# Gated linear attention and a token/channel mixer on one core: batch 0's mixer input made directly in transposed form, residuals joined on TensorE, and a new instruction order

## The chip, the core and the metric

The kernel runs on one core of a Trainium2 chip. The metric is the device time of one execution in microseconds (us); lower is better. The input is the same draw in every run.

## The reference

Two stages follow each other. The first is a gated recurrence with a state of 48 x 48 for each of 4 batches and 8 heads, over 768 steps:

```python
state = alpha[:, :, t, :, None] * state + k[:, :, t] (outer) v[:, :, t]
y[:, :, t] = q[:, :, t] @ state
```

The outputs of the 8 heads are laid side by side, so that each batch has an x of 768 tokens x 384 channels. The second stage is a mixer on each batch:

```python
xt = x.transpose(0, 2, 1)
h = np.maximum(xt @ w_tok1, 0.0) @ w_tok2          # 768 -> 256 -> 768, over tokens
u = x + h.transpose(0, 2, 1)
h2 = np.maximum(u @ w_ch1, 0.0) @ w_ch2            # 384 -> 1536 -> 384, over channels
return u + h2
```

All inputs and the output are float32; the matmuls run in bfloat16.

## The kernel before

**Tiling.** The recurrence is computed in blocks of 256 tokens: 3 blocks for each batch, 12 in all, numbered 0 to 11. A block puts pairs of neighbouring tokens on the 128 partitions. For each block the kernel loads alpha, k, q and v (`ld_at`, `ld_kt`, `ld_qt`, `ld_vt`, 384 KB each), takes logarithms and cumulative sums (`ln`, `cum`/`cumw`), exponentials (`E`, `IE`), scales k and q (`kk`, `qq`, L702), transposes them on TensorE (`trk`, `trq`, L717 or L721) and evicts them to SBUF (`evk`, `evq`), multiplies keys by queries (`G0`, `G1`, L651), applies the causal mask (`mask0`, `mask1`, L771, VectorE), and multiplies by v (`y`). What earlier tokens contribute through the carried state comes in as two small groups of matmuls into the same two PSUM banks, `ia` and `ib`. Between them stands a fence (`fe`, L823): ScalarE or VectorE copies four numbers out of the banks. In the kernel before the order in a block is `y`, `ia`, `fe`, `ib`; then the two 128-token halves are evicted as x (`x0`, `x1`). The state itself goes through `K` (TensorE), `sa` (VectorE) and `sm` (VectorE or GpSimd).

**Mixer of a batch.** `t1` (12 matmuls of 128x384, L843), relu (`ht`), `t2` (L850; for batch 0 with one identity matmul on x ahead of each pair, L848, which is how the residual enters; for the other batches the residual is added by VectorE, L854), eviction of u (`u`), transposes of u (`up`, 18 of 128x128, L861), their eviction (`ut`), then 24 groups of three matmuls (`c1`, L869) with a relu each (`rt`), then 24 groups of three (`c2`, L874), the residual sum (`o`, L878, VectorE) and the store (`st`).

**Order.** The instruction order is not found by a scheduler at build time. The string `ORDER` lists every operation once, with a letter for its engine (t TensorE, s ScalarE, v VectorE, g GpSimd, y SyncE's DMA queue, n left out); each engine runs its own operations in that order. A planner (`Plan.decode`) walks the list with estimated durations only to hand out buffers and PSUM banks, so a bank's next writer waits for the reader that the planner put before it. Operations whose names begin with `f` and a digit, and `pad`, are matmuls on zeros that compute nothing. They can be left out (n) or kept (t).

**Weights.** w_tok1, w_tok2, w_ch1 and w_ch2 come in pieces of 384 KB (`ldw_wt1`, `ldw_wt2`, `ldw_wc1`, `ldw_wc2`; L620), interleaved with the loads of the blocks on the one SyncE queue, and each is cast to bfloat16 (`cw_...`, L759 or L758). The mixer of batch 0 cannot start a stage before its weights are cast.

**Shared port.** VectorE and GpSimd operations that share a port are chained by a dependency (`shared`, L745).

Of the kernel before, what the change touches and what calls it, by code (L numbers as in the profile page):

```python
# [9 lines left out]
BF16 = mybir.dt.bfloat16  # L10
# [53 lines left out]
class Plan:  # L64
# [29 lines left out]
    def decode(self):  # L94
# [9 lines left out]
        dma_in, ring = 2500.0, [0.0] * 3  # L104
# [5 lines left out]
        for o in self.order:  # L110
# [61 lines left out]
            if o.dma is not None:  # L172
                kind, dur, lead, tail = o.dma
                s = max(st + lead, dma_in)
                dma_in = s + dur * (1.0 if s < 16000.0 else LATER)
                o.end = dma_in + tail + (lag(s) if kind == "i" else 0.0)
                if kind == "i":
                    ring = ring[1:] + [dma_in]
                    free[e] = max(free[e], ring[0] - 600.0)
# [19 lines left out]
LATER = 1.06  # L199


def lag(s):
    return (0.0 if s < 12500.0 else 600.0 if s < 14000.0 else 1600.0 if s < 20000.0 else 2400.0 if s < 30000.0 else
            3300.0 if s < 58000.0 else 1500.0)

# [6 lines left out]
IN_NS, WT_NS, OUT_NS = 1250.0, 1020.0, 580.0  # L212
# [4 lines left out]
    "tpk": 2, "tpq": 2, "gtm": 2, "tmp": 3, "ss": 5, "x": 14, "ht": 4, "u": 13, "ut": 2, "rt": 24, "o": 3,  # L217
}
WIDE = (0, 1, 2)
JOIN = (0,)  # L220
# [6 lines left out]
def build(g):  # L227
# [8 lines left out]
    def attention(n):  # L236
# [31 lines left out]
        else:  # L268
# [15 lines left out]
        kk = O("kk", either(dve(768), pool_tt(768)), 5, writes=[pkk], reads=[kt, IE], port=True, preds=k_in + [e2],  # L284
               emit=lambda e: g.scaled(e, pkk, kt, IE, wide))
        qq = O("qq", either(dve(768), pool_tt(768)), 5, writes=[pkq], reads=[qt, E], port=True, preds=q_in + [e1],
               emit=lambda e: g.scaled(e, pkq, qt, E, wide))
# [4 lines left out]
        bk, bq, tpk, tpq = V(kind), V(kind), V("tpk"), V("tpq")  # L292
        shape = [128] * 8 if full else [64] * 8
        trk = O("trk", pe(shape), 8, writes=[bk], reads=[pkk], preds=[kk] + fill("trk", bk),
                emit=lambda e: g.tr(bk, pkk, full, 2, 1), mode=mode, mm=8 if full else 16)
        trq = O("trq", pe(shape), 8, writes=[bq], reads=[pkq], preds=[qq] + fill("trq", bq),
                emit=lambda e: g.tr(bq, pkq, full, 2 if full else 1, 1 if full else 4), mode=mode,
                mm=8 if full else 16)
        evk = O("evk", either(dve(1024, True), act(1024)), 9, writes=[tpk], reads=[bk], preds=[trk],
                emit=lambda e: g.trev(e, tpk, bk, full))  # L300
        evq = O("evq", either(dve(1024), {"ACT": (1190.0, 1310.0)}), 9, writes=[tpq], reads=[bq], preds=[trq],
                emit=lambda e: g.trevq(e, tpq, bq, full))
        gtm = V("gtm")
        masks = []
        for sl in range(2):
            gp = V("pair")
            G = O(f"G{sl}_", pe([128] * 4), 10 + sl, writes=[gp], reads=[tpk, tpq], preds=[evk, evq] + fill(f"G{sl}", gp),
                  emit=lambda e, sl=sl, gp=gp: g.gmm(gp, tpk, tpq, sl, full), mode="G", mm=16)
            masks.append(O(f"mask{sl}_", dve(1024), 12 + sl, writes=[gtm], reads=[gp], preds=[G],
                           emit=lambda e, sl=sl, gp=gp: g.mask(gtm, gp, sl)))  # L310
        nst = 2 if k < NB - 1 else 1
        kp = V("pair")
        KO = O("K", {"PE": (276.0 if nst == 2 else 140.0, 420.0)}, 9.5, writes=[kp], reads=[pkk, vb], preds=[kk, vc] + fill("K", kp),
# [3 lines left out]
        for hf in range(nst):  # L317
# [4 lines left out]
            else:  # L322
# [7 lines left out]
        yi = O("y", pe([48] * 16), 14, writes=[yp], reads=[gtm, vb], preds=masks + [vc] + fill("y", yp),  # L330
               emit=lambda e: g.ymm(yp, gtm, vb), mode="R", mm=32)
        use = [st for st in states[:2] if st]
        ia = O("ia", pe([48] * 4), 15, writes=[yp], reads=[tpq] + [v for v, _ in use], preds=[yi] + [o for _, o in use],
               emit=lambda e: g.inter(yp, tpq, [st and st[0] for st in states[:2]], 0, full), mode="R", mm=8)
        fe = O("fe", either(act(4), dve(4)), 15, reads=[yp], preds=[ia], emit=lambda e: g.fence(e, yp))
        io = O("ib", pe([48] * 4), 15, writes=[yp], reads=[tpq] + [v for v, _ in use], preds=[fe],
               emit=lambda e: g.inter(yp, tpq, [st and st[0] for st in states[:2]], 1, full), mode="R", mm=8)
        for hf in range(2):
            x = V("x")
            xo = O(f"x{hf}_", either(act(384), dve(384)), 16, writes=[x], reads=[yp], preds=[io],  # L340
                   emit=lambda e, hf=hf, x=x: g.xev(e, x, yp, hf))
            xs[(b, 2 * k + hf)] = (x, xo)
# [12 lines left out]
    def mixer(b):  # L355
# [20 lines left out]
        us = []  # L376
        for i in range(NS):
            bank, u = V("one"), V("u")
            add = b in JOIN
            o = P.op(f"t2_{b}_{i}", pe([384] * (3 if add else 2)), m0 + (1900 + 330 * i) * sc, writes=[bank],  # L380
                     reads=[h for h, _ in hts] + ([x[i][0]] if add else []),
                     preds=[h for _, h in hts] + [wl[("wt2", z)] for z in range(2)] + ([x[i][1]] if add else []),
                     emit=lambda e, i=i, bank=bank, add=add: g.tok2(bank, i, [h for h, _ in hts], add and x[i][0]),
                     mm=3 if add else 2)
            uo = P.op(f"u_{b}_{i}", either(act(384), dve(384)) if add else dve(384), m0 + (1950 + 330 * i) * sc,
                      writes=[u], reads=[bank] + ([] if add else [x[i][0]]), preds=[o],
                      emit=lambda e, i=i, bank=bank, u=u, add=add:
                      g.xev(e, u, bank, 0) if add else g.uadd(u, bank, x[i][0]))
            us.append((u, uo))
        ut = V("ut")  # L390
        uts = []
        for p in range(3):
            bank = V("one")
            o = P.op(f"up_{b}_{p}", pe([128] * 6), m0 + (3900 + 340 * p) * sc, writes=[bank],
                     reads=[us[2 * p][0], us[2 * p + 1][0]], preds=[us[2 * p][1], us[2 * p + 1][1]],
                     emit=lambda e, p=p, bank=bank: g.utr(bank, us[2 * p][0], us[2 * p + 1][0]), mm=6)
            eo = P.op(f"ut_{b}_{p}", either(dve(768, True), act(768)), m0 + (3950 + 340 * p) * sc, writes=[ut],
                      reads=[bank], preds=[o], emit=lambda e, p=p, bank=bank: g.utev(e, ut, bank, p))
            uts.append(eo)
        rts = []  # L400
        for mc in range(NDC):
            rt = V("rt")
            ro = []
            for half in range(2):
                bank = V("one")
                o = P.op(f"c1_{b}_{mc}_{half}", pe([384] * 3), m0 + (4900 + 975 * mc + 487 * half) * sc, writes=[bank],
                         reads=[ut], preds=uts[0:2 + half] + [wl[("wc1", mc // 2)]],
# [5 lines left out]
        for i in range(NS):  # L413
# [4 lines left out]
            for tag, c0, c1 in [("", 0, 256), ("b", 256, HD)] if last and i == 0 else [("", 0, HD)]:  # L418
                bank, prev, n = V("one"), None, c1 - c0
                late = 9900.0 * (last and i == 0) + 400.0 * (c0 > 0)  # L420
                for q4 in range(4):
# [4 lines left out]
                                emit=lambda e, q4=q4, c0=c0, c1=c1, bank=bank, i=i: g.ch2(bank, i, q4, rts, c0, c1))  # L426
                oo = P.op(f"o_{b}_{i}{tag}", dve(n), at + (2000 + late) * sc, writes=[o_],
                          reads=[bank, us[i][0]], preds=[prev],
                          emit=lambda e, c0=c0, c1=c1, bank=bank, i=i, o_=o_: g.oadd(o_, bank, us[i][0], c0, c1))
# [25 lines left out]
f1G1_1n ld_at0y pad64_t pad32_n f1cumw_2n f0cumw_0n f1G0_0n f2trk_0n f2cumw_0n f2G0_0n f1cumw_0n ln0s cumw0t  # L455
f2trq_2n f1G0_1n f0cumw_2n f1cumw_1n f1G1_0n ld_at1y ln1s pad16_t ld_kt0y f0trq_0n f0cumw_1n f2G1_1n f2G1_0n
f2cumw_1n cumw1t f1trk_0t IE0s kk0v ld_qt0y E0s qq0v E1s Et1s f2K_0n f2y_1n ld_qt1y qq1v f0trk_0n f0K_1n f0G0_0n
f2trq_1n f1trq_1n f0K_2n ld_kt1y f0trq_2n ld_vt0y ld_at2y Et0s f0trq_1n f1trk_1n f0K_0n ld_vt1y trk0t f1trq_0t
IE1s f2G0_2n f2trq_0n ld_qt2y trq0t evq0s ld_kt2y f2trk_1t trq1t f0trk_1t ldw_wt10y ld_vt2y f1trk_2n f0y_0n kk1v
evk0v f0G1_1n trk1t ld_at3y ld_kt3y f2K_2n f2trk_2n evq1s vb0g ldw_wt11y ld_qt3y evk1v ldw_wt21y f1y_1n f0G1_2n  # L460
f2G0_1n G0_0t mask0_0v f0G1_0n G1_0t f1K_0n K0t f0G0_1n G0_1t f2y_2n f0y_1n s0_0v sa1_0v f0trk_2n f1trq_2n
mask1_0v f2cumw_2t f1K_1n sm1_0g ln2s cumw2t vb1g f2G1_2n f1y_0n G1_1t mask0_1v ldw_wt20y mask1_1v E2s f2y_0n
y0t ia0t fe0s ib0t Et2s x0_0s IE2s f0G0_2n f2K_1t K1t f0y_2n x1_0s qq2g trq2t ldw_wc15y ldw_wc14y sa0_1v sm0_1v
# [62 lines left out]
class Emit:  # L526


    def __init__(self, tc, ctx, q, k, v, alpha, w, out):
# [48 lines left out]
        for t, base in ((self.mk, 0), (mkb, 128)):  # L578
            gp.affine_select(out=t, in_=t, compare_op=ALU.is_ge, fill=0.0, base=base,
                             pattern=[[-1, 2], [1, 128]], channel_multiplier=-2)  # L580
# [352 lines left out]
```

## Time and profile before

| what | value |
|---|---|
| median of 5 runs | 171.29 us (170.55 to 172.52) |
| profiled execution, its own time | 171.29 us |
| its span (first to last instruction) | 169.6 us; 1.7 us lie around it |
| TensorE busy | 161.4 us (95%) |
| VectorE / ScalarE / GpSimd busy | 118.6 / 88.2 / 55.8 us |
| HBM read / written | 25.17 MB / 4.72 MB |

PE is TensorE's matmul side, PEld its weight loads, DVE VectorE, ACT ScalarE, POOL GpSimd, SP and SPq SyncE and its DMA queue. "L651" is line 651 of the kernel. A busy TensorE is counted from the start of a matmul to its modelled end; matmuls overlap, so that a stage of small matmuls can look busy while it is not at its peak. "PEclk" is the share of the full TensorE clock that was granted. The view by windows gives busy time by engine in a stretch; the chain is followed back from the last instruction to what released each step.

### The profile page before, as it was taken

How to read it: one execution, taken by the hardware profiler on the slowest of the kernel's cores; microseconds unless marked ns; L12 is line 12 of the kernel's file. 1: busy time of each engine (PE TensorE's matmuls, PEld its weight loads, DVE VectorE, ACT ScalarE, POOL GpSimd, SP SyncE). 2: the span in 40 equal slices, each digit the busy share in tenths (PEclk: the TensorE clock that was granted, in tenths of full speed). 3: DMA queues.
4: the chain of work that ended last, by engine and by line, in shares of the span. 5: the costliest groups of instructions: out<-in, count | busy, mean ns of one | idle time of the engine just before them, and what ended most of it. 6: DMA issues, size and time to landing. Idle time of an engine off the chain costs nothing.

```text
span 169.6 us, 5827 instructions
## 1 busy us (share of the span) xinstructions
PE 161.4 (95%) x2511; PEld 105.1 (62%) x2511; DVE 118.6 (70%) x212; ACT 88.2 (52%) x170; POOL 55.8 (33%) x65
## 2 busy tenths in 40 slices
PE   7868988999999999999999999999999999999993
PEld 7535655766666666756666766756666666666562
DVE  4369678798798586999988849878974526632342
ACT  3871697758875725775657792485242413310100
POOL 5004464503651157554796459702000000000000
PEclk9997899999999999999999999999999999999999
DMA  5999999999999999989972950030000000013323
GB/s 137 325 288 274 295 289 357 309 305 253 339 346 295 268 269 272 296 221 285 271 198 58 314 152 0 4 139 4 2 4 4 0 0 0 0 50 139 139 93 139
DMA packets 58777, 30.25 MB, mean 178 GB/s; under 512 B 50688, under 2 KB 58496, under 8 KB 58752
## 3 DMA queue, kind: packets, MB, share of 16 engines
q1 hardware_dynamic: 57888, 28.78, 59.2%
q10 hardware_dynamic: 864, 1.11, 1.8%
q8 instruction: 19, 0.31, 0.7%
q14 instruction: 6, 0.05, 0.1%
HBM read 25.17 MB, written 4.72 MB: 176 GB/s over the span
## 4 chain that ended last, share of the span: by engine, by line
PE 87%; DMA 3%; DVE 3%; SPq 3%; issue 1%; ACT 0%; DVEq 0%
PE ps L869 28%; PE ps L874 28%; PE ps L651 14%; PE ps L843 5%; PE ps L850 5%; DMA ld<-in_k_dram 3%; SPq L605 3%; PE ps L717 2%; PE ps L861 2%; PE ps L721 2%; DVE pkk L702 1%; DVE gtm L771 1%; PE ps L848 1%; DVE u L759 0%; ACT IE L683 0%
## 5 line engine op out<-in xcount | busy, mean ns | idle before, releaser
L874 PE MATMUL ps<-wc,rt 128*128 128x384 bf16 (+2 forms) x300 | 52.6, 320 | 0.0
L869 PE MATMUL ps<-ut,wc 128*128 128x384 bf16 x288 | 51.7, 326 | 0.0
L838 ACT ACTIVATE rt<-ps 128x384 bf16<-128x384 f32 x53 | 24.6, 494 | 27.2 <-PE ps L869 27.0
L874 PEld LDWEIGHTS <-rt 128*128 128x128 bf16 x300 | 28.1, 98 | 16.8
L869 PEld LDWEIGHTS <-wc 128*128 128x128 bf16 x288 | 26.8, 98 | 16.8
L771 DVE TENSOR_TENSOR gtm<-ps,mk 128x1024 bf16<-128x1024 f32 x24 | 28.7, 1218 | 3.8 <-PE ps L651 3.7
L840 DVE TENSOR_SCALAR rt<-ps 128x384 bf16<-128x384 f32 x43 | 22.1, 551 | 10.2 <-PE ps L869 10.0
L878 DVE TENSOR_TENSOR o<-ps,u 128x384 f32<-128x384 f32 (+2 forms) x25 | 13.1, 539 | 12.8 <-PE ps L874 10.1
L702 POOL TENSOR_TENSOR pkq<-ld,E 128x768 bf16<-128x768 f32 x7 | 12.7, 1812 | 6.0 <-DVE ld L698 4.0
L800 POOL TENSOR_TENSOR ss<-tmp,E 128x192 bf16<-128x192 f32 x12 | 6.1, 507 | 23.7 <-DVE tmp L797 14.5
L651 PE MATMUL ps<-zs 128*128 128x64 bf16 (+1 forms) x100 | 10.6, 268 | 1.8 <-DVE zs L571 1.1
L854 DVE TENSOR_TENSOR u<-ps,x 128x384 bf16<-128x384 f32 x18 | 9.2, 552 | 3.3 <-PE ps L850 3.1
L758 ACT COPY tpq<-ps 128x1024 bf16<-128x1024 bf16 x8 | 10.4, 1316 | 1.7 <-PE ps L721 1.3
L702 DVE TENSOR_TENSOR pkk<-ld,IE 128x768 bf16<-128x768 f32 x7 | 6.7, 956 | 6.2 <-ACT IE L686 3.9
L850 PE MATMUL ps<-ht,wt 128*128 128x384 bf16 x48 | 10.4, 326 | 0.0
L758 ACT CAST x<-ps 128x384 bf16<-128x384 f32 x18 | 8.1, 485 | 2.9 <-PE ps L651 2.9
L759 POOL CAST wc<-ld 128x768 bf16<-128x768 f32 x8 | 6.5, 826 | 7.9 <-DVE ld L636 4.5
L702 POOL TENSOR_TENSOR pkk<-ld,IE 128x768 bf16<-128x768 f32 x5 | 9.0, 1808 | 0.1
L843 PE MATMUL ps<-x,wt 128*128 128x384 bf16 x48 | 9.0, 327 | 0.0
L651 PE MATMUL ps<-tpq,tpk 48*64 48x128 bf16 x384 | 8.7, 221 | 0.1
L694 POOL TENSOR_TENSOR ld<-ld,ld 128x384 f32<-128x384 f32 x7 | 7.0, 999 | 4.8 <-DVE ss L800 2.9
L651 PEld LDWEIGHTS <-tpk 48*64 48x64 bf16 x384 | 6.3, 108 | 2.2 <-issue 1.5
(88 smaller groups left out, 212.6 us busy)
## 6 DMA issues: line engine op xcount, KB each, us to landing
ld<-in_alpha_dram SPq DMA_DIRECT2D x12, 384.0 KB, 5.8
ld<-in_k_dram SPq DMA_DIRECT2D x12, 384.0 KB, 5.8
ld<-in_q_dram SPq DMA_DIRECT2D x12, 384.0 KB, 5.3
ld<-in_moe_w_ch_dram SPq DMA_DIRECT2D x12, 384.0 KB, 6.1
out_dram<-o SPq DMA_DIRECT2D x18, 192.0 KB, 2.5
ld<-in_v_dram SPq DMA_DIRECT2D x14, 192.0 KB, 4.8
ld<-in_v_dram SPq DMA_DIRECT2D x5, 384.0 KB, 5.9
ld<-in_moe_w_tok_dram SPq DMA_DIRECT2D x4, 384.0 KB, 6.1
```

The costliest lines, as they stand in the source:

```text
L651: return self.pe.matmul(out, lhsT=lhsT, rhs=rhs, start=start, stop=stop, skip_group_check=True)
L702: self.shared(self.eng[e].tensor_tensor(self.t(dst)[:, :, :, 0:D], self.t(src).rearrange("p h s d -> p s h d"), bass.AP(tensor=f.tensor, o ...
L758: return self.act.copy(d, s)
L771: self.nc.vector.tensor_tensor(self.t(gtm)[:, sl, :, :], self.pair(gp).rearrange("p a (j t) -> p (a j) t", t=128), bass.AP(tensor=m.tensor ...
L838: self.act.activation(d, s, AF.Relu)
L840: self.nc.vector.tensor_scalar_max(d, s, 0.0)
L843: self.pe.matmul(self.bank(bank)[:, 0:HD], lhsT=self.wt1[:, kc, m * 128 : m * 128 + 128], rhs=self.t(x), start=(kc == 0), stop=(kc == NS - 1))
L850: self.pe.matmul(self.bank(bank)[:, 0:HD], lhsT=self.wt2[:, kc, i * 128 : i * 128 + 128], rhs=self.t(hts[kc]), start=(kc == 0 and not x), ...
L854: self.nc.vector.tensor_tensor(self.t(u), self.bank(bank)[:, 0:HD], self.t(x), ALU.add)
L869: self.pe.matmul(self.bank(bank)[:, 0:HD], lhsT=self.wc1[:, kc, mc * 128 : mc * 128 + 128], rhs=self.t(ut)[:, kc, half * 384 : half * 384 ...
L874: self.pe.matmul(self.bank(bank)[:, 0 : c1 - c0], lhsT=self.t(rts[mc][0])[:, i * 128 : i * 128 + 128], rhs=self.wc2[:, mc, c0:c1], start=( ...
L878: self.nc.vector.tensor_tensor(self.t(o)[:, c0:c1], self.bank(bank)[:, 0 : c1 - c0], self.t(u)[:, c0:c1], ALU.add)
```

## The change

Five things change together.

1. **Batch 0's u is made transposed.** For each of six pieces (half of the tokens, 128 channels) a bank gets three identity matmuls on x (`xt`), which put x transposed into it, and then two matmuls with the roles of the operands exchanged (`t2`: the hidden tile is the stationary operand, w_tok2 the moving one). One eviction writes `ut` at once. The six joins on L848, the 18 transposes `up` and the three evictions `ut` of batch 0 go away.
2. **Batch 0's second residual is joined on TensorE.** Three identity matmuls (`cr`) put u back upright into the bank in which `c2` then accumulates; `o` becomes a plain copy, which ScalarE may do as well.
3. **Carried state first.** In each block the order becomes `ib`, `fe`, `ia`, `y`, where it was `y`, `ia`, `fe`, `ib`.
4. **Block 2 in head halves.** Scaling, transposes, evictions, `G`, mask and `y` of block 2 are cut by heads instead of by token slots, so that the second half of a step overlaps the first half of the next. The number of mask operations and of matmuls stays the same; kk, qq and the evictions become twice as many of half the size.
5. **A new order** for all engines, planned with other transfer rates and delays, with another choice of zero matmuls: 12 of 128x512 instead of 20; 80 of 128x64 as before.

The core of the diff:

```diff
-LATER = 1.06
+LATER = 1.1
-IN_NS, WT_NS, OUT_NS = 1250.0, 1020.0, 580.0
+IN_NS, WT_NS, OUT_NS = 1215.0, 1050.0, 580.0
-JOIN = (0,)
+DIRECT = (0,)
+SPLIT = (2,)
...
-        yi = O("y", pe([48] * 16), 14, writes=[yp], reads=[gtm, vb], preds=masks + [vc] + fill("y", yp), ...
-        ia = O("ia", pe([48] * 4), 15, ... preds=[yi] + [o for _, o in use], ...
-        fe = O("fe", either(act(4), dve(4)), 15, reads=[yp], preds=[ia], ...
-        io = O("ib", pe([48] * 4), 15, ... preds=[fe], ...
+        ib = O("ib", pe([48] * 4), 12, ... preds=[z[1] for z in evs] + [o for _, o in use] + fill("y", yp), ...
+        fe = O("fe", either(act(4), dve(4)), 13, reads=[yp], preds=[ib], ...
+        ia = O("ia", pe([48] * 4), 13, ... preds=[fe], ...
+        yi = None
+        for hh, tg in parts:
+            yi = O("y" + tg, pe([48] * (16 // len(parts))), 14, writes=[yp], reads=[gtm, vb],
+                   preds=(masks if hh is None else [masks[hh]]) + [vc, fe] + ([yi] if yi else []), ...
...
+    def xt(self, bank, j, xs):
+        for z, x in enumerate(xs):
+            self.mm(self.bank(bank)[:, z * 128 : z * 128 + 128], self.t(x)[:, j * 128 : j * 128 + 128], self.idn, z == 0,
+                    False)
+
+    def tok2t(self, bank, half, j, hts):
+        for kc in range(NDT):
+            self.mm(self.bank(bank)[:, 0:HD], self.t(hts[kc])[:, j * 128 : j * 128 + 128],
+                    self.wt2[:, kc, half * 384 : half * 384 + 384], False, kc == NDT - 1)
+
+    def utd(self, e, ut, bank, half, j):
+        self.copy(e, self.t(ut)[:, j, half * 384 : half * 384 + 384], self.bank(bank)[:, 0:HD])
+
+    def resid(self, bank, ut, i):
+        for j in range(NM):
+            self.mm(self.bank(bank)[:, j * 128 : j * 128 + 128], self.t(ut)[:, j, i * 128 : i * 128 + 128], self.idn, j == 0,
+                    False)
```

The first part of the order, by engine, up to the first `t2` of batch 0. The first line of each pair is before, the second after; `f2K_1` is three zero matmuls, `f1...` two, `f0...` one.

```
TensorE before: pad64 cumw0 pad16 cumw1 f1trk_0 trk0 f1trq_0 trq0 f2trk_1 trq1 f0trk_1 trk1 G0_0 G1_0 K0 G0_1 f2cumw_2 cumw2 G1_1 y0 ia0 ib0 f2K_1 K1 trq2 y1 ia1 trk2 ib1 t1 f1G0_2 G0_2 f1K_2 K2 G1_2 t1 x3 cum3 f1y_2 y2 ia2 ib2 t1 x8 trk3 trq3 t2
TensorE after:  pad64 cumw0 f0trk_0 f0G0_0 cumw1 pad16 f1trq_1 trq0 f2trk_0 trk0 trq1 trk1 G0_0 G1_0 K0 G0_1 cumw2 f2K_1 K1 f1y_0 G1_1 ib0 ib1 ia0 y0 trk0_2 cum3 K2 y1 ia1 trk1_2 trq0_2 trq1_2 t1 x3 G0_2 t1 x2 ib2 G1_2 t1 x3 xt_2 y0_2 ia2 y1_2 xt_0 trk3 xt_1 t1 x4 trq3 xt_3 xt_5 t2
VectorE before: kk0 qq0 qq1 kk1 evk0 evk1 mask0_0 s0_0 sa1_0 mask1_0 mask0_1 mask1_1 sa0_1 sm0_1 kk2 sa1_1 fe1 evk2 mask0_2 sa0_2 mask1_2 kk3 fe2 x1_2 qq3 cw_wt20
VectorE after:  kk0 qq0 qq1 kk1 evk0 evk1 mask0_0 s0_0 sa1_0 mask0_1 P3 sa0_1 mask1_0 sa1_1 mask1_1 evk0_2 fe1 qq0_2 sa0_2 qq1_2 cw_wt10 x0_1 evk1_2 evq1_2 mask0_2 mask1_2 q0r3 qq3 evk3 ht_0_1
DMA before: at0 at1 kt0 qt0 qt1 kt1 vt0 at2 vt1 qt2 kt2 wt10 vt2 at3 kt3 wt11 qt3 wt21 wt20 wc15 wc14 wc10 at4 qt4 wc11 wc13 wc12 kt4 at5 vt3
DMA after:  at0 at1 kt0 qt0 qt1 kt1 vt0 at2 vt1 at3 kt2 vt2 qt2 wt10 kt3 wt11 qt3 wt21 wt20 wc15 wc10 at4 wc14 wc11 wc13 wc12 qt4 vt3 kt4 at5
```

## The prediction

> **What bounds the kernel now.** I read the page first, for which engine is full and when; then the windows, to cut the span into stages; then the chain of waits around the point where TensorE stops waiting; then the timeline and the load queue at that point. The page:
>
> ```profile
> span 169.6 us, 5827 instructions
> ...
> PE 161.4 (95%) x2511; PEld 105.1 (62%) x2511; DVE 118.6 (70%) x212; ACT 88.2 (52%) x170; POOL 55.8 (33%) x65
> ...
> PE   7868988999999999999999999999999999999993
> ...
> PEclk9997899999999999999999999999999999999999
> ```
>
> TensorE has holes in the first eighth only; from about 34 us it is full to the end. The windows (columns: length, then busy time and count of PE, PEld, DVE, ACT, POOL, then granted clock, DMA share, GB/s):
>
> ```profile
> 15.00:18.20 3.20, 3.15 (x27) 1.64 (x30) 2.88 (x4) 0.20 (x1) 1.27 (x2) 0.50 1.08 314
> 18.20:30.60 12.40, 11.02 (x299) 7.20 (x287) 9.43 (x15) 10.30 (x21) 6.51 (x7) 1.00 1.04 318
> 30.60:35.50 4.90, 4.80 (x72) 3.33 (x70) 3.58 (x6) 2.99 (x5) 2.48 (x3) 1.00 1.04 309
> 35.50:167.00 131.50, 131.35 (x1909) 84.40 (x1906) 94.54 (x168) 65.43 (x133) 42.46 (x40) 1.00 0.52 150
> ```
>
> From 35.5 to 167 us TensorE is busy 131.35 of 131.50, and the view of waits lists none for it after 30.6. So the end is one sum: the start of batch 0's t2 (30.6), plus all TensorE work that stands after it, plus the last eviction and store (2.7). VectorE's 94.5 of 131.5 decides nothing there. Between 15.0 and 18.2 the clock is half. The chain at the hinge:
>
> ```profile
> 28.14 0.27 PE ps L651 x8
> 28.41 1.41 PE ps L843 x8
> 29.82 0.94 PE ps L717 x16
> 30.76 0.16 PE ps L848
> ...
> 34.80 0.42 PE ps L651 x16
> 35.22 0.44 PE ps L861 x6
> 35.66 0.49 PE ps L869 x3
> ```
>
> A 384-wide matmul takes its turn in 0.163 us, six 128-wide in 0.34 (0.057 each). What t2 waits for at 30.6:
>
> ```profile
> 29.12 0.96 DVE L702 TENSOR_TENSOR pkq<-ld,E 128x768 bf16<-128x768 f32 x1
> 29.58 0.88 ACT L838 ACTIVATE ht<-ps 128x384 bf16<-128x384 f32 x2
> 30.00 0.56 DVE L759 CAST wt<-ld 128x768 bf16<-128x768 f32 x1
> ```
>
> The hidden tile is ready at 30.46, the second piece of w_tok2 (wt20) at 30.56. Its load (the second of two):
>
> ```profile
> L620 SPq DMA_DIRECT2D ld<-in_moe_w_tok_dram x2: 432/953/1474, 21.5 to 23.0; - x2
> ...
> DMA to landing us min/median/max: 6.2/6.4/6.7
> ```
>
> Issued at 23.0 and 6.2 on its way, it lands at 29.2. That is a floor for t2, whatever the engines do.
>
> **What the Trainium skill says.** "TensorE: Matmul & The Clock Gate", Part 1 (the HAM clock gate): TensorE's clock halves after a window of about 3.4 us with too little activity and returns after a busy one. The trace agrees: half clock for about 3.4 us, after a window in which TensorE was busy some 1.9 us of 3.4. The same page, Back-to-back issue gap, prices a 128-wide matmul at about 56 ns when warm; the row above gives 57. "PSUM — Partial Sum Buffer", The four PSUM rules: the first matmul of a group clears the accumulate bits of the whole bank it writes, and a seed should go in by an identity matmul. That is how `xt` and `cr` work, and why they cost TensorE turns; no trace of before can show more of it than L848.
>
> **The change, part by part.** All of it is measured from t2's start, since everything after is TensorE work in one queue.
>
> *u transposed, residual joined.* Removed after t2's start: six joins, 6 x 0.163 = 0.98, and 18 transposes, 18 x 0.057 = 1.02. The t2 matmuls keep number and width. Added: 18 `xt` and 18 `cr` of 128 columns. Nothing in the trace is exactly such a matmul; the transposes of the same shape are the nearest row, and I take 0.057 for both (with full weight reloading 0.098, the length of an LDWEIGHTS, it could not be more than 1.76 for 18). In the new order 15 of the 18 `xt` stand ahead of t2, where TensorE has holes, and 3 after: 0.17. `cr` adds 1.02. Sum: -0.98 - 1.02 + 0.17 + 1.02 = -0.81. The three ut evictions of batch 0 (0.55 and twice 0.80) and three of six o sums leave VectorE's or the common load; worth nothing by itself, as TensorE sets the pace. It does shorten the way from t2 to the first c1: five pairs 1.63, G of block 3 0.84 with two changes of tile shape 0.2, 0.17, 0.33: c1 starts at about 33.4, not 35.5, and 1.02 of these 2.1 is paid back in `cr`.
>
> *Changes of tile shape.* Each costs about 0.1 (six L869 take 1.08 behind small matmuls, 0.97 otherwise). Counted in the orders behind t2: 45 before, 46 after: +0.1.
>
> *When t2 starts: the load.* The first 19 transfers are the same set in both orders, with wt20 the nineteenth, and the ring was never short of issues. Its landing stays at 29.2; I allow 0.5 either way. Its cast goes to GpSimd (0.82, as its other 128x768 casts), which is idle then: 30.05. Before, it stood behind qq3 on VectorE.
>
> *When t2 starts: block 2.* Up to mask0_0 both orders run alike (13.8 to 15.0), the half clock included, because the idle stretch at 11 to 12.5 (waiting for k of block 1, which lands at 11.5) stays. Then cumw2 comes directly at 15.05 instead of after three zero matmuls (1.23 at half clock), done at 16.7. Three zero matmuls ahead of K1 (1.23) and K1 (0.45) bring 18.45. From there VectorE has no hole; start to start: sa 0.30, mask 1.16, sa 0.30, mask 1.16, evk half 0.36, fence 0.1 give 21.9. qq halves must follow GpSimd's sm: 22.0. Then qq 0.46, sa 0.29, qq 0.46, cast 0.49, x 0.49, evk 0.35, evq 0.64, two masks 2.32: 27.5. (Halves are taken as half of the streaming part plus the fixed part of the full rows, 0.96, 0.69 and 1.31.) q of block 2 lands three places later, at about 21, and is not the last. y of the second head half and two ScalarE evictions bring x at 29.05, last t1 29.4; before, these ended at 29.8. Then trq3 0.45 and two `xt` 0.34 on TensorE: 30.2. VectorE has q0r3, qq3, evk3 (0.49, 0.90, 0.63) ahead of the relu (0.56): 30.15. So three ends meet at 30.05 to 30.2, and t2 starts at about 30.3: -0.3. If TensorE falls to half clock again in the window from 21.6 (in my walk it is busy 2.35 of 3.4 us in the one before; 1.9 lost the clock above, nothing between is shown), t2 comes about 0.3 later. If the clock is never lost, block 2 is a microsecond sooner, and only the load's 30.05 is left.
>
> *Carried state first.* Takes a fence round trip from behind the last mask and puts it ahead. For blocks 3 to 11 it gains nothing in a full TensorE. A fence that isn't covered costs 0.23 to 0.34 (19.06 to 19.29, and the wait at 28.14); in the new order one c1, a transposition or another block's group stands between `ib` and `ia` or `y` nearly everywhere. Cost 0, bounds 0 to 0.3 a block.
>
> *Stalls behind t2.* Before has none, so this can only lose. In my walk the tightest points are c1_0_7_1 (cast of wc13 on ScalarE ready at 38.3, wanted at 38.25) and some banks freed 0.1 to 0.2 ahead. Taken: 0.2; bounds 0 and 1.0.
>
> Sum: -0.3 - 0.81 + 0.1 + 0.2 = -0.8. The profiled execution took 171.29 with a span of 169.6, and 171.29 is also the median: 170.5.
>
> **The rivals.**
> - *The load comes sooner or the clock stays* (0.20). Queue order and rates changed, and wt20's landing is the floor. If it lands a microsecond sooner and the clock holds, t2 starts at about 29.3: -1.3 - 0.8 + 0.1 and no stalls, 169.3. For: rates in the head vary (248 GB/s at 11 to 15, 314 after). Against: the same bytes ahead of it.
> - *Given back* (0.13). Tighter banks and casts cost what the shorter work gains: about 171.3.
> - *Fences exposed* (0.12), the slower one. `fe` is in the queue of VectorE or ScalarE; where a mask of 1.22 stands ahead of it, `ia` and `y` wait in TensorE's queue, and all mixer work behind them. Nine blocks; from 0.11 each the change loses, from 0.3 each it is over 1% slower; at 0.4 each, 3.6 - 1.0 = +2.6, 173.9. For: VectorE is 70% busy, more in the middle. Against: the two exposed fences cost 0.3, and work stands between.
>
> **How the numbers follow.** The forecast, 170.5, has 0.55. About 1% (1.7 us) can be told from no change. Faster than 169.6 is most of the first rival and a little of the forecast's edge: 0.22. Slower than 173.0 is the third rival: 0.12. The rest, 0.66. The range, 169.0 to 172.5, holds the load 0.5 early and late, stalls up to 1.0 and half of the first rival's tail.
>
> **What would show it.** Right: t2 at 30.0 to 30.6; first c1 near 33.4; no L848; TensorE full from t2 on; its end near 166.1. Wrong: waits of TensorE for casts, fences or banks after 33 us; t2 behind 31; `xt` or `cr` at well over 57 ns each; half clock between 20 and 30 us.

## The result, and the profile after

The changed kernel took 170.08 us in the median (169.24 to 172.58, 26 runs), the kernel before 171.28 us (48 runs on the same chip). The ratio is 0.9947, with a 95% interval of 0.9926 to 0.9969: 0.9 us of 171.29 less, 0.5 to 1.3. The ratios leave out runs more than 1.5% above the fastest of the same kernel (3 of the 27 here, the profiled execution counted), so they are not the quotient of the two medians. The time is within 1% of before, as forecast (170.5, chance 0.66 for "within 1%"). The profiled execution took 170.02 us with a span of 168.3, 1.27 less than that of before. From its page:

```profile
PE 159.9 (95%) x2515; PEld 104.5 (62%) x2515; DVE 115.1 (68%) x208; ACT 88.1 (52%) x174; POOL 57.7 (34%) x67
...
PE   7858899999999999999999999999999999999993
PEclk9997799999999999999999999999999999999999
```

TensorE is again full after the first eighth, and the half clock stands in the same slices. The windows (length, then busy time and count of PE, PEld, DVE, ACT, POOL, then granted clock, DMA share, GB/s):

```profile
15.00:18.20 3.20, 2.98 (x23) 1.20 (x27) 2.38 (x5) 2.08 (x4) 0.51 (x1) 0.52 1.12 303
18.20:30.60 12.40, 11.15 (x309) 7.99 (x310) 11.24 (x20) 8.02 (x18) 7.23 (x9) 0.99 0.96 298
30.60:35.50 4.90, 4.90 (x62) 3.00 (x61) 4.90 (x7) 3.64 (x7) 2.46 (x3) 1.00 1.11 352
35.50:166.00 130.50, 130.06 (x1910) 83.80 (x1908) 88.69 (x158) 64.98 (x134) 44.13 (x42) 1.00 0.52 152
```

From 30.6 on TensorE has no hole, and the view of waits lists none for it there. VectorE is now full from 30.6 to 35.5 (4.90 of 4.90), and TensorE never waits for it there. The chain at the hinge:

```profile
20.03 5.79 DMA ld<-in_moe_w_tok_dram
...
26.75 0.48 PE ps L890 x2
27.23 1.11 PE ps L684 x46
28.35 0.45 PE ps L751 x8
28.80 0.17 PE ps L684 x3
28.96 0.65 PE ps L890 x4
29.61 0.45 PE ps L751 x8
30.06 3.13 PE ps L684 x53
```

L890 is `t1`, L751 is `trk3` and later `trq3`, L684 holds `y`, `ia`, `xt`, `t2` and G of block 3. The first `t2` starts at 30.23, the first `c1` at 33.02 (before: 30.60 with its join, and 35.50). From 26.73 on TensorE goes from matmul to matmul without a hole, so `t2` itself waits for nothing but TensorE's own queue; the last `xt` stands 0.06 us ahead of it. By the timeline:

```profile
25.85 0.83 ACT L799 CAST wt<-ld 128x768 bf16<-128x768 f32 x1 [0.98 <-DMA ld<-in_moe_w_tok_dram]
26.73 0.50 PE L890 MATMUL ps<-x,wt 128*128 128x384 bf16 x2 [0.37 <-ACT junkACT L799]
29.17 0.82 POOL L800 CAST wt<-ld 128x768 bf16<-128x768 f32 x1 [1.69 <-DVE pkq L736]
29.62 0.55 DVE L887 TENSOR_SCALAR ht<-ps 128x384 bf16<-128x384 f32 x1
29.65 0.49 ACT L885 ACTIVATE ht<-ps 128x384 bf16<-128x384 f32 x1
```

The cast of wt20 ends at 29.99, 0.24 ahead of `t2`; it had waited for VectorE's `qq3` (the shared port), which ended at 29.10, not for the load. The two relus end at 30.17 and 30.14, just in time. What lies further back is the first line: the load of **wt11**, the second piece of w_tok1. Its cast ends at 26.68, and `t1` starts at 26.73, after TensorE sat idle for 0.37. (The view names the fence copy that ran right behind the cast on ScalarE; but `t1` doesn't read it, and in e1 and e5 to e8 as well this `t1` starts 0.05 to 0.06 after the cast's end.) Block 2's masks end only 0.06 us later than this path needs them: at 27.64, for the second half of `y` at 27.70, 0.97 behind that `t1`, where in e5 it is 0.91. So two paths meet there, and wt20 is not one of them. The instructions of the loads' line, from 20 to 24 us (durations, first and last start, and the time from issue to landing):

```profile
L653 SPq DMA_DIRECT2D ld<-in_moe_w_tok_dram x3: 662/1006/1750, 20.0 to 23.4; - x3
...
DMA to landing us min/median/max: 5.6/5.8/6.2
```

The first is wt11: issued at 20.0, it lands at 25.82. The last is wt20: issued at 23.4, it lands 5.6 later, at 29.04, where before it landed at 29.2.

**A second reading of the times: the clock.** Each run comes with its mean TensorE clock, to about 0.01. One window of 3.4 us at half clock in a span of 168 us makes 1 - 0.5 x 3.4/168 = 0.990, so 1.00, 0.99, 0.98 and 0.97 tell how many windows a run lost in the head, the only place where the profiles show half clock while TensorE has work. The median of the runs (and their number; the two rows are from two chips):

| kernel | none lost | one lost | two or three lost |
|---|---|---|---|
| before (runs beside e5 to e8) | 170.29 (35) | 171.26 (24) | - |
| after | 169.63 (10) | 170.05 (10) | 171.50 (7) |

So the same program loses none to three windows from run to run. The change is worth 0.7 us where none is lost and 1.2 where one is, and one lost window goes with 0.97 more before and 0.42 more after (there the two groups overlap: 169.24 to 170.42 and 169.62 to 171.92). The clock doesn't explain every difference: before without a lost window had 170.29, 170.31 and 170.36 beside e5 to e8, e1 to e4 and e9 to e11, but 171.74 (20 runs) beside e12. The two profiled executions, on which the prediction's sum was made, had one each. Below, differences against after are given by the ratios to before (after: 0.9947) and, where there are enough runs, between runs that lost the same number of windows.

### The profile page after: what moved, and what is told of

Read it like the earlier page. It is cut to its first block, busy times and chain, and to the rows that moved or that the text cites. A ratio compares the mean times of both kernels' runs of the same rounds, so it can differ in the third digit from the quotient of the medians.

```text
span 168.3 us, 5840 instructions
## 1 busy us (share of the span) xinstructions
PE 159.9 (95%) x2515; PEld 104.5 (62%) x2515; DVE 115.1 (68%) x208; ACT 88.1 (52%) x174; POOL 57.7 (34%) x67
## 3 DMA queue, kind: packets, MB, share of 16 engines
q10 hardware_dynamic: 864, 1.05, 1.7%
## 4 chain that ended last, share of the span: by engine, by line
PE 82%; SPq 11%; DMA 3%; issue 1%; DVE 0%; ACT 0%
PE ps L684 41%; PE ps L932 29%; SPq L638 9%; PE ps L890 4%; PE ps L895 3%; DMA ld<-in_moe_w_tok_dram 3%; PE ps L755 2%; PE ps L924 2%; SPq L653 2%; PE ps L751 2%; DVE o L941 0%; ACT junkACT L799 0%; ACT wt L799 0%
## 5 line engine op out<-in xcount | busy, mean ns | idle before, releaser
L684 PE MATMUL ps<-wc,rt 128*128 128x384 bf16 (+2 forms) x300 | 53.1, 320 | 0.0
L885 ACT ACTIVATE rt<-ps 128x384 bf16<-128x384 f32 x58 | 26.9, 496 | 25.4 <-PE ps L932 25.4
L684 PEld LDWEIGHTS <-rt 128*128 128x128 bf16 x300 | 27.9, 98 | 16.2
L932 PEld LDWEIGHTS <-wc 128*128 128x128 bf16 x288 | 26.8, 98 | 17.3 <-DVE wc L800 0.4
L887 DVE TENSOR_SCALAR rt<-ps 128x384 bf16<-128x384 f32 x38 | 19.7, 552 | 11.8 <-PE ps L932 11.6
L941 DVE TENSOR_TENSOR o<-ps,u 128x384 f32<-128x384 f32 (+2 forms) x19 | 10.0, 533 | 10.8 <-PE ps L684 10.8
L736 POOL TENSOR_TENSOR pkk<-ld,IE 128x768 bf16<-128x768 f32 (+1 forms) x9 | 14.6, 1634 | 4.5 <-ACT ut L799 3.4
L799 ACT COPY tpq<-ps 128x1024 bf16<-128x1024 bf16 (+1 forms) x9 | 11.2, 1248 | 4.9 <-DVE vb L800 3.5
L890 PE MATMUL ps<-x,wt 128*128 128x384 bf16 x48 | 9.3, 327 | 0.4 <-ACT junkACT L799 0.4
L736 POOL TENSOR_TENSOR pkq<-ld,E 128x768 bf16<-128x768 f32 x5 | 9.1, 1811 | 0.6 <-ACT E L713 0.4
L684 PE MATMUL ps<-zs 128*128 128x64 bf16 (+1 forms) x92 | 8.1, 258 | 1.1 <-DVE zs L603 1.1
L684 PE MATMUL ps<-tpq,tpk 48*64 48x128 bf16 x384 | 8.7, 219 | 0.0
L842 DVE TENSOR_TENSOR tmp<-ps,ss 128x192 f32<-128x192 f32 x16 | 5.7, 355 | 4.2 <-PE ps L684 3.1
L800 DVE COPY tpk<-ps 128x1024 bf16<-128x1024 bf16 (+1 forms) x12 | 7.6, 642 | 1.0 <-PE ps L755 0.8
L736 DVE TENSOR_TENSOR pkq<-ld,E 128x768 bf16<-128x768 f32 (+1 forms) x8 | 6.9, 857 | 1.5 <-ACT E L713 0.8
L800 POOL CAST vb<-ld 128x768 bf16<-128x768 f32 x5 | 4.1, 826 | 10.8 <-DMA ld<-in_v_dram 9.6
```

Of the source, the lines that this page charges most:

```text
L684: return self.pe.matmul(out, lhsT=lhsT, rhs=rhs, start=start, stop=stop, skip_group_check=True)
L736: self.shared(self.eng[e].tensor_tensor(self.t(dst)[:, :, h0:h1, 0:D], self.t(src)[:, h0:h1].rearrange("p h s d -> p s h d"), bass.AP(tens ...
L799: return self.act.copy(d, s)
L800: return self.shared(self.eng[e].tensor_copy(d, s))
L885: self.act.activation(d, s, AF.Relu)
L887: self.nc.vector.tensor_scalar_max(d, s, 0.0)
```

## The experiments

All are edits of the kernel after, but for e9, e10 and e12, which are edits of the kernel before. Lines of code move by a few between them.

**e1: the load of wt20 two transfers later.**

```diff
-ldw_wt20y ... ldw_wc15y ... ldw_wc10y
+ldw_wc15y ldw_wc10y ldw_wt20y
```

> The load of the second w_tok2 piece (wt20) is moved two transfers later in the queue, behind wc15 and wc10; nothing else changes. Theory (the end is t2's start plus the TensorE work behind it, and wt20 is a floor for t2): wt20 lands two transfers of about 1.15 us later, at about 31.3 us, its cast takes 0.82, t2 starts at 32.2 to 32.4 and not at 30.23, and the end moves by the same 2.0 to 2.2 us: about 172.2. Rival (the later stages have slack and catch up, or the load is not the floor): the end moves by under 1 us, below 171.1.

171.63 us, ratio 1.0078 [1.0049, 1.0108]: 1.3%, 2.2 us, more than after (171.49 against 169.63, 1.86, with no window lost). In the view of waits from 28 to 34 us TensorE has one line:

```profile
PE ps L684 <- POOL wt L800: 1.9, 1, 1.9
```

The hidden tile was ready early (this run lost no window, the last `t1` started at 28.60), and `t2` started at 31.61, right behind the cast's end at 31.56. That is less late than expected (32.2), because wt20 landed at 30.61. Against after's profile `t2` is 1.38 later and the end 1.75. So a late wt20 does hold `t2`, and what stands behind it adds in full. It does not show that wt20 held `t2` in after, where its cast was done 0.24 ahead. The other 0.37 are two gaps, 0.26 and 0.10, between `t2` matmuls of batch 2 near 105 us, which after's profile doesn't have.

**e2: each `cr` matmul twice**, 18 more behind `t2`.

```diff
-        for j in range(NM):
+        for j in list(range(NM)) * 2:
             self.mm(self.bank(bank)[:, j * 128 : j * 128 + 128], self.t(ut)[:, j, i * 128 : i * 128 + 128], self.idn, ...
```

> Each cr of batch 0 (three identity matmuls of 128 columns that put u back upright) is issued twice, so 18 more such matmuls stand behind t2; the result is the same. Theory (TensorE is full behind t2 and nothing hides work there): 18 x 0.057 = +1.03 us, about 171.1; by the length of a weight load, 0.098 each, at most +1.76. Rival (there is slack behind t2, other engines set the pace): under +0.3 us.

170.92 us, ratio 1.0026 [0.9995, 1.0056]; among runs with no lost window 170.68 (10 runs) against 169.63: 1.05 us more. From `t2` to TensorE's end it took 136.45 against 135.33: 1.12. Of this 1.00 stands at the 18 added matmuls themselves, 0.056 from start to start, and 0.12 elsewhere (0.10 of it at one `y` at 90 us). A matmul of 128 columns lasts 0.22 from start to modelled end, but they overlap; the step from start to start is what the queue pays. `cr` costs what was assumed, and the rival, slack behind `t2`, is out.

**e3: parts 1 and 2 undone in the new order**: joins, upright u, transposes and `ut` evictions back in place of `xt`, `t2` transposed and `cr`.

```diff
-DIRECT = (0,)
+DIRECT = ()
+JOIN = (0,)
```

> Parts 1 and 2 are undone in the new order: batch 0's u is made upright with one identity matmul ahead of each pair, transposed by 18 matmuls and evicted three times more; xt and cr are gone; the o of batch 0 is a sum on VectorE again. Carried state first, the head halves and the rest of the order stay. Theory (these parts are worth the TensorE work that they take from behind t2): +0.98 + 1.02 - 0.17 - 1.02 = +0.81 us, t2 itself within 0.3 us of 30.2, c1 about 2 us later: about 170.9. Rival (the gain is the order's, the transposed u is neutral): within 0.2 us of 170.1.

172.20 us, ratio 1.0094 [1.0055, 1.0134]: 1.5%, 2.5 us, more than after, three times the sum. The trace parts it: from the first `t2` on 137.28 against 135.33, 1.95 more (and 1.86 more in the timed runs with no window lost, 4 of them). Of this 0.74 is the work (five joins and 18 transposes against 18 `cr` and three `xt`; one join stands ahead of that `t2`), and four gaps that after does not have come to 1.5 (0.53 at 32.9, then 0.30, 0.40 and 0.30); the rest goes the other way. The one at 32.9 stands in the view of waits:

```profile
PE ps L689 <- DVE ut L805: 0.4, 1, 0.4
```

There G of block 3 waits for a bank that an eviction of `ut` gives back (ended 33.43, G at 33.49). That this order has too little other work to put between the longer form's steps is my reading of it. So the number prices the form in this order, not the work alone.

**e4: block 2 whole** (part 4 undone), and **e11: the same, with nine more zero matmuls in the head** (e5's edit).

```diff
-SPLIT = (2,)
+SPLIT = ()
```

> Part 4 alone is undone: block 2 is scaled, transposed, evicted and masked whole (one kk on GpSimd, one qq and one evk on VectorE, one evq of 1.31 us on ScalarE), the mask by token slots; the rest of the order stays, except that ib of block 2 stands behind its second G. Theory (t2 is set by the chain of block 2 on VectorE, with the load of wt20 just under it): the eviction of q is later and longer, the second mask ends at about 28.1 and not 27.6, t2 starts at 30.7 to 30.9 and not 30.23, the end moves by +0.5 to +0.6 us: about 170.7. Rival (the load alone sets t2): no change within 0.2 us. Rival (head halves only cost operations): 0.2 us or more faster.

> Block 2 whole as in e4, with the nine zero matmuls of e5 ahead of trq0 and trk1. Theory (most of e4's 2.7 was lost clock, since all four of its runs lost one to three windows): with the clock kept, t2 at 30.2 to 30.7 and the ratio 0.996 to 0.999, which is part 4's own price of 0.1 to 0.6 against e5's 0.9953. Rival (the chain of whole block 2 is itself 2 us longer): t2 at 31.5 or later at full clock, ratio 1.006 or more.

e4: 172.26 us, ratio 1.0105 [1.0064, 1.0146], 2.7 us more than after instead of 0.5. All four runs lost one to three windows. The clock of the profiled one, from its page:

```profile
PEclk9996569999999999999999999999999999999999
```

Half clock from 14.2 to 24.4, and `t2` at 32.19; behind it 135.89, 0.56 more than in after, most of it one gap of 0.40 near 36 us. In e11 9 of 22 runs lost none and 10 lost one. Its match is e5 below, which has the same zeros and block 2 in halves: 169.99 against 169.78 with none lost (not clear of the scatter), 171.08 against 170.30 with one, and by the ratios (0.9983 [0.9959, 1.0007] against 0.9953) 0.5 us. So part 4 is worth 0.2 to 0.8 us beside e5's zeros, about what the theory had. In e4 it is more: like with like, 1.1 to 1.6 over after (four runs in all), and the rest of its 2.7 is that every run lost windows. Whether whole blocks lose the clock more often four runs can't tell.

**e5: nine more zero matmuls** of 512 columns in holes of the head, three ahead of `trq0` and six ahead of `trk1`, and **e6: five fewer**, those ahead of `K1` and `G1_1`.

```diff
-f2trq_0n f0trk_1n f1trk_1n f2trk_1n
+f2trq_0t f0trk_1t f1trk_1t f2trk_1t      (e5)
-f2K_1t f1y_0t
+f2K_1n f1y_0n                            (e6)
```

> Nine more zero matmuls of 512 columns in holes of the head where TensorE only waits: three (0.64 us) ahead of trq0 and six (1.28 us) ahead of trk1, where it stood idle for 0.84 and 1.28 us. Theory (the clock of the head decides part of the time): no window before 25 us has less than 2.4 us of work in 3.4, so the clock stays full, cumw2 to K1 takes 1.2 us less, t2 starts at 29.2 to 30.0 and never at 31 or later; the median falls to 0.990 to 0.992 of the kernel before (after: 0.9947), and the runs at 171 and more, of which after has 8 in 27, are gone. Rival (the holes cost nothing, the chain of block 2 and the load set t2): within 0.1 of after, 0.9945, and scattered like it; at worst 0.2 later where a zero matmul outlasts the hole.

> The five zero matmuls of 512 columns between cumw2 and G1_1 are left out (three ahead of K1, two ahead of G1_1). Rival (chain): K1 is 1.2 to 1.4 us earlier, VectorE's chain of block 2 gets ahead by the 1.25 it waited for K1, t2 falls back on the load, 29.9, so 0.3 less than after: 0.993. Theory (clock): the window from 18.5 loses 0.43 to 1.4 of its 2.4 us of work, a second window at half clock follows in many runs, the chain then takes 0.5 to 1.5 longer than in after, and the median is 0.996 to 1.003 of the kernel before, with more runs at 171 and above.

Both theories came out half right. e5: 170.14 us, ratio 0.9953 [0.9931, 0.9976], so no faster. The clock did what was expected: 15 of 22 runs lost no window, 7 lost one, none more. But the runs without loss are at 169.78, no better than after's 169.63. Its profile, with a full clock throughout, shows why. Block 2's masks are done 0.2 earlier than in after, but wt11 lands at 25.75 (25.82 in after), and TensorE waits for its cast as before:

```profile
PE ps L889 <- ACT junkACT L798: 0.4, 1, 0.4
```

From this `t1`, at 26.66, to `t2`, at 30.09, it is 3.43 us; in e6 and e7 3.43 too, and 3.50 in after, where the masks ended last. So with the clock kept the load of wt11 is what is left. wt20's cast ended at 29.95, 0.14 ahead of `t2`; in e1, where `t2` did wait for it, the distance is 0.05. And behind `t2` this run has the same two gaps as e1's: 135.70, 0.37 more than after. There VectorE's masks of a later block end 0.2 later than in after; what delayed them was not tried.

e6: 170.27 us, ratio 0.9976 [0.9955, 0.9996], 0.3% more than after, with intervals that overlap. No run kept the clock: 3 lost one window, 14 two, 5 three. The windows of its profile show how (columns as above: the busy time of TensorE follows the length, its clock stands third from the end):

```profile
13.90:17.30 3.40, 2.20 (x104) 1.63 (x92) 3.30 (x6) 2.71 (x5) 0.51 (x1) 1.00 1.04 272
17.30:20.70 3.40, 2.23 (x72) 1.87 (x62) 3.02 (x6) 2.29 (x6) 2.58 (x4) 0.51 1.07 309
```

A window with 2.20 us of work in 3.40 is followed by half clock, here until 24.2. And yet block 2's masks are done at 27.41, as in e5 (27.45): five zero matmuls less in the chain (1.07 us at full clock) pay for two lost windows. `t2` starts at 30.11, again 3.43 behind the `t1` that waits for wt11's cast (landed 25.77). So in after these zeros buy a clock that they then spend themselves; they are worth 0.3% at most.

**e7: carried state last again in blocks 3 to 11**, with nothing between.

```diff
-ib3t fe3s c1_0_2_0t ... y3t ia3t
+c1_0_2_0t ... y3t ia3t fe3s ib3t        (so for 3 to 11)
```

> Part 3 undone in blocks 3 to 11, with nothing between: y, ia, fence, ib stand directly behind one another at the place where after has ia or y. Theory: the fence's round trip (TensorE's last write, 8 elements by VectorE or ScalarE, the semaphore back) is then open behind each y at 0.25 to 0.35 us, nine times, less where two blocks stand together: 2.0 to 3.0 us more behind t2 than in after, ratio to the kernel before 1.007 to 1.012. Rival (the round trip is small against the queue of matmuls and partly runs beside their ends): under 0.1 each, ratio 0.995 to 1.000.

174.86 us, ratio 1.0219 [1.0157, 1.0281]: 4.7 us more than after, twice the expected. The waits from 33 us on:

```profile
PE ps L694 <- DVE junkDVE L810: 1.4, 5, 0.3
PE ps L694 <- ACT junkACT L809: 1.2, 4, 0.4
PE ps L694 <- DVE gtm L827: 0.9, 1, 0.9
```

Nine fences and one mask, 3.5 us as the view counts them. From start to start, the last matmul of `ia` and the first of `ib` lie 0.43 to 0.57 us apart, 4.2 for nine, some 4.0 more than if they followed one another. The view counts from the modelled end of the last matmul, 0.18 us after its start, though without a fence the next one starts some 0.02 after it. "TensorE: Matmul & The Clock Gate", Single matmul latency, gives (398 + N)/2.4 ns for a matmul on the full array, 186 for N = 48; an end that is modelled is no test of that. The copy is 0.16, and the rest goes on the way there and back. The 0.9 is a mask that now stood behind a waiting fence in VectorE's queue.

**e8: carried state last in block 2 alone.**

```diff
-ib2t ... fe2s y0_2t ia2t ... y1_2t
+... y0_2t ... y1_2t ia2t fe2s ib2t
```

> Part 3 undone in block 2 alone: y0, y1, ia, fence, ib. Theory: in the chain of the head the round trip comes behind the last mask, 0.3 for the fence and 0.1 for ib, so x of block 2 comes 0.3 to 0.4 later and t2 with it, 30.5 to 30.7 at one window of half clock, against 30.23; nothing changes behind t2. Ratio 0.996 to 0.998. Rival: the load (cast done 29.99) and the relu hide it: t2 at 30.2 to 30.3, ratio 0.9947.

170.22 us, ratio 0.9976 [0.9950, 1.0002], 0.3% or 0.5 us more than after, as the theory had it; 169.87 against 169.63 with no window lost, 170.67 against 170.05 with one. None of these is clear of the scatter by itself. The timeline of e8 (start, duration; masks of block 2, fence, eviction of x):

```profile
24.37 2.35 DVE L826 TENSOR_TENSOR gtm<-ps,mk 128x1024 bf16<-128x1024 f32 x2
...
27.49 0.16 ACT L808 COPY junkACT<-ps 128x4 f32<-128x4 f32 x1 [1.37 <-PE ps L693]
...
28.02 0.86 ACT L808 CAST x<-ps 128x384 bf16<-128x384 f32 x2 [0.36 <-PE ps L693]
```

and of after:

```profile
25.30 2.34 DVE L817 TENSOR_TENSOR gtm<-ps,mk 128x1024 bf16<-128x1024 f32 x2
...
28.11 0.86 ACT L799 CAST x<-ps 128x384 bf16<-128x384 f32 x2 [1.37 <-PE ps L684]
```

e8's profiled run kept the clock and had its masks done 0.92 earlier (26.72 against 27.64), but x came only 0.09 earlier: 1.30 from the last mask to x instead of 0.47, of which 0.72 are `ia`, fence and `ib`. wt11 had landed early (25.27), and from the `t1` behind its cast to `t2` it is 3.96 here, 0.53 more than in e5 to e7. So part 3's gift to the head is 0.8 behind the masks, 0.5 at `t2` in this profile, and 0.2 to 0.6 in the time, as far as the scatter lets one say.

**e9: the kernel before with five more zero matmuls** ahead of `trk1`.

```diff
-f1trk_1n ... f2K_0n
+f1trk_1t f2K_0t
```

> The kernel before with five more zero matmuls of 512 columns (1.07 us) in the 1.43 us in which TensorE waits for kk1 ahead of trk1; nothing else. Theory (the clock of the head): the window that ends near 14.8 has then 3.0 instead of 1.9 us of work, half clock disappears in most runs, and the runs of before that lost one window (24 of 59 at 171.26, against 170.29 for those that lost none) move to 170.3: ratio 0.995 to 0.998, as much as the whole change or nearly. Rival (in before, too, the load sets t2, so the clock costs nothing): 1.000.

170.68 us, ratio 0.9990 [0.9962, 1.0017]: no difference. The clock was kept in 21 of 22 runs, and `t2`'s first join came at 29.27 instead of 30.60, so the rival's number came without its reason. But on this chip only 12 of 43 runs of the kernel before lost a window, so that at 0.95 each there were 0.27 us to be had, and the runs with full clock were at 170.53 against 170.36. The profiled one, at 172.64, had a stall of 1.9 us behind `t2` (at 65 us, for a sum `o` that itself waited for a store), so where the difference went in the timed runs is open. The number that I had expected counted on the other chip's share of lost windows.

**e10: parts 1 and 2 alone, in the order of before**, and **e12: the same with the order mended.**

```diff
-JOIN = (0,)
+DIRECT = (0,)
...
-ht_0_0s qq3v trk3t evk3s trq3t cw_wt20v t2_0_1t t2_0_3t ...
+ht_0_0s xt_0_3t xt_0_4t qq3v trk3t evk3s trq3t cw_wt20v t2_0_1t t2_0_2t ... u_0_3v evq3v ... xt_0_5t t2_0_5t G0_3t   (e10)
+... evq3v u_0_4s u_0_3s ... c1_0_9_0t c1_0_8_0t G0_3t rt_0_9_0s mask0_3v ...                                          (e12)
```

> Parts 1 and 2 alone, in the order of before: xt, t2 transposed, cr; carried state last and whole block 2 as before. Three xt stand in waits of block 2, two ahead of trk3, one behind t2. Theory (TensorE work behind t2 decides): six joins 0.98 and 18 transposes 1.1 less, one xt 0.19 and 18 cr 1.12 more, so 0.8 less behind t2 (135.5 against 136.27), t2 at 30.6 or 0.1 to 0.3 later for the two xt ahead of trk3: ratio 0.995 to 0.997, and 169.5 to 169.9 where no window is lost. Rival (as in e3, an order made for the other form adds waits): behind t2 136.2 or more, ratio 1.000 or above.

> Parts 1 and 2 alone again, with e10's order mended where its trace waited: evq3 is not kept behind u_0_3 on VectorE's queue, u_0_3 goes to ScalarE, G and masks of block 3 stand behind two c1 groups, rt of mc 8, 9 and first half of 1 go to ScalarE. Theory (the work saved is 0.8 to 0.9 and e10's 3.4 us of waits were of its order): behind t2 135.4 to 135.8, ratio 0.995 to 0.999; t2 itself comes up to 0.3 later than in before for the two xt ahead of trk3. Rival (the form itself brings the waits, through the transposed tile that needs all of a half's u before the first c1): over 1 us of waits behind t2 stays, ratio 1.003 or more.

e10: 173.91 us, ratio 1.0174 [1.0137, 1.0212], slower. Behind `t2` 138.92, with these waits:

```profile
PE ps L669 <- DVE tpq L777: 1.5, 1, 1.5
PE ps L903 <- DVE rt L858: 0.9, 1, 0.9
PE ps L903 <- DVE gtm L789: 0.5, 1, 0.5
```

The gaps themselves are 1.62, 0.66 and 1.09 from start to start, 3.4 in all; without them it would be 135.5, next to after's 135.33. e12: 171.55 us, ratio 0.9999 [0.9970, 1.0027]; in its profiled execution, which at 173.11 was 1.6 over the median, behind `t2` 137.55, with other waits, the longest:

```profile
PE ps L903 <- POOL wc L777: 0.9, 1, 0.9
```

The first `c1` is now ready before its weights: `c1_0_9_0` needs wc14, the second of the w_ch1 loads, whose cast began at 33.46, and starts at 34.35. The new order loads wc10 ahead of wc14 and begins with the `c1` of mc 0. So the saved work is there in both (with the gaps of 3.4 and 1.6 taken out, 135.5 and 135.9), and neither order lets it through; a price in us of parts 1 and 2 alone was not got, and the theory's expectation for e12 failed (behind `t2` it had 135.4 to 135.8).

## Why the prediction was right

- **The sum was the right one.** `t2` 0.37 earlier (30.60 to 30.23), 0.92 less from there to TensorE's last end (136.25 to 135.33): 1.29, which is the 1.27 by which the profiled executions differ. e1 and e2 moved each of the two terms by itself, and the time followed.
- **`t2`'s start** was forecast at 30.3 and came at 30.23, half by the path that was named. Block 2 went as forecast: masks done at 27.64 (forecast 27.5), x at 28.97 (29.05), relus at 30.17 and 30.14 (30.15), TensorE's queue of `trq3` and `xt` at 30.23 (30.2). The load did not: the prediction's floor was wt20, and wt20 had 0.2 to spare. The load that met the masks, within 0.06 us, was wt11, which the prediction never named; it landed at 25.82 (24.92 in before, where its cast came only at 27.24). So the forecast for a clock that is never lost, with only the load's 30.05 left, came true in number (e5, 30.09) by luck: another load set it, and block 2's masks were 0.2 (e5) to 0.5 (e7) sooner, not a microsecond.
- **Work behind `t2`.** Forecast -0.81. Summed in the two traces from start to start: joins -0.98, transposes of u -1.10 (0.061 each, not 0.057), `cr` +1.01, `xt` +0.18: -0.89. The step stands.
- **Changes of tile shape and stalls** were the mis-sized terms: +0.1 and +0.2 forecast. All that is left behind `t2`, -0.92 less -0.89, is -0.03. TensorE's waits are nil in after's profile; e1 and e5, with the same order behind `t2`, show 0.37, so the 0.2 was no bad guess for other executions. One more change of tile shape cost nothing: the 672 small matmuls of `y`, `ia`, `ib` and `K` took 9.1 us before and 8.8 after, and the other groups 0.3 more. Why was not tried. These 0.3 are most of the difference between the forecast -0.8 and the profile's -1.27.
- **Carried state first at no cost**: right, no fence is waited for behind `t2`. But the price of an uncovered fence was too low: 0.41 to 0.55 more than without one (e7), not 0.23 to 0.34. And for block 2 no gain was set apart, while e8 shows some 0.5 at `t2`; it lies within the forecast start of `t2`.
- **The rivals.** "The clock stays", 169.3, is no other fate of the kernel but a share of its runs: 10 of 27 lost no window, at 169.63. "Given back" is what e12 shows for parts 1 and 2 in the old order. "Fences exposed" did not come; e7 shows what nine of them would have cost, 1.0219.
- **What stays open.** How the 0.37 at `t2` divides among parts 3, 4 and 5 is not shown: e4, e8 and e11 take back one part each, in runs whose loads and clock moved too.

## What to carry to other kernels

Where one engine is full behind a point, price a change as the shift of that point plus the work behind it, and measure both in the trace; here they gave 1.29, where the two executions differ by 1.27. A shorter path lets the next need come sooner, so its loads, casts and queue places must move with it: the same saving was worth nothing or cost 3 us in orders made for the longer path. When the point has moved, follow it back in the new trace: here the load that had been watched was no longer near the end of the chain, and another was. Before crediting an edit of a short head with a microsecond, sort the runs by granted clock.

## What the hardware showed that was not expected

- **The half clock falls differently in each run.** The edges of its 3.4 us windows lay elsewhere in each profile: the half clock began at 14.2 (e4), 14.8 (before), 15.1 (after), 17.3 (e6) or 20.5 (e2). "TensorE: Matmul & The Clock Gate", Part 1, says the window is free-running and does not restart with the kernel; the traces agree. In the table above the runs of after that lost windows took 0.4 to 1.9 us more.
- **How much work keeps the clock.** Taking the windows from the first edge on, and the busy time with its modelled ends, one with 1.8 to 1.9 us of work in 3.4 lost it (before, after, e4, e2), and one with 2.4 or more kept it; between, both occur: 1.98 (e1) and 2.26 (after) kept it, 2.20 (e6) and 2.35 (e11) lost it.
- **The load moves too.** In profiles with a full clock and the same queue order, wt11 landed at 25.0 (e3), 25.3 (e8), 25.4 (e7) and 25.8 us (e5), and wt20 at 28.1, 28.3, 28.5 and 29.0. In e7 and e5, with the same order from there to `t2`, `t2` moved with wt11: 29.73 and 30.09. So the floors under `t2` scatter by 0.7 to 0.9 us themselves; why was not tried.
